# Moving the early weight loads behind ScalarE gates, the warming products onto a zero block, and one fence copy to ScalarE, in a fused linear-attention and MLP kernel

## The chip, the cores and the metric

The kernel runs on one core of a Trainium2 chip. The metric is the device time of one execution in microseconds (us); a profile's span runs from the first to the last instruction of the profiled execution. TensorE is called PE here, VectorE DVE, ScalarE ACT, GpSimd POOL and SyncE SP, as in the profile.

## The reference

Two blocks, one behind the other, all in float32. The first is a recurrence over 768 tokens for 4 batches and 8 heads of 48 channels; the second is an MLP on the 3072 resulting rows of 384 values, with a gate of erf(softplus).

```python
for t in range(S):
    cur = einsum('bhd,bhe->bhde', u * k[t], v[t])
    y[:, :, t] = einsum('bhd,bhde->bhe', r[t], state + cur)
    state = w[t][..., None] * state + einsum('bhd,bhe->bhde', k[t], v[t])
x = y.transpose(0, 2, 1, 3).reshape(B * S, H * D)   # 3072 x 384
h = x @ w_in                                        # 384 x 2048
g = h * erf(log(1 + exp(h)))
out = g @ w_out                                     # 2048 x 384
```

## The kernel before, in words

The work is cut into 12 steps. A step is 128 tokens of two batches: 16 (batch, head) units, kept as 8 pairs on 128 partitions. The order of the instructions on all five engines is written out by hand (`tc.manual_schedule`); each engine runs its own list strictly in that order, and a semaphore is waited for where data or a buffer comes from another engine.

Within a step the token-by-token recurrence is done by halving: for each of six levels PE makes 64 small products (L718, `level_products`) of scaled r and k, DVE scales the halves of r and k in place by the running products of w (L358 and L365, `scale`; step 0 has its own last form, L377), and the masked result is put into `own` (L728 and L735 `take_level`; in step 0 L983, L749 and L1022). The running products of w are made by POOL (L403). Then `own` times v is added into the PSUM tile `y` (L762, `from_own`, once per `swap`), with a small copy of `y` between the two calls as a fence (`fence`, L771, into `seen`). k is transposed by PE, copied to `kT` (L1047 in step 0, L1172 later) and multiplied by v for the state; `middle` is the state after half a step (L1056, L1192, L1196). `through_state` adds r times state (L788), and brings `y` to the MLP's input `xT`: in step 0 by way of `y3` (L797), three products with a placement matrix (L804, the function `hop`) and three ACT copies (L810); in step 1 by copies (L816) and small DMAs (L822).

The MLP of step s-1 runs on PE between the levels of step s. `hidden` makes two blocks of the hidden layer per piece, 12 records of x times w_in (L1268), and ACT copies them out of PSUM (L1277); there are two PSUM buffers for that. Piece n needs the n-th pair of blocks of w_in.

The weights are float32 numbers that come as 64-bit words and are converted on the way: 8 pairs of blocks for w_in, then 8 for w_out, numbered 0 to 15. `convert` gives each pair five stages:

- `l`, `load`: two DMAs of 384 KB by SP (L181) into one of three `words` buffers. With an argument `behind`, one element is first written into the buffer from that tile, by ACT (L273) or POOL (L275), and the DMA waits for it: this is the gate.
- `b`, `scale_high` on ACT (L290, for w_out L292), which for pairs from 2 on uses the PSUM tile `y` as scratch; `r`, `scale_low` on ACT (L298) into `rest`.
- `h`, `shift` on DVE (L307, for w_out also L312), and `o`, `add` on POOL (L320). `j` is `h` and `o` together.

`send(what)` runs the next pair through the named stages, with a counter for each stage. In step 1 it is called behind the first level's products and then at `place(n)`, which stands behind each level, by the row of `CONVERT` for the step.

Before the change the loads stand so: pair 0 at the start, pair 1 in step 0 at level 4 behind a POOL gate, pairs 2 and 3 and v of step 1 at the end of step 0 behind `seen` and `middle` on ACT, pair 4 in `hop`, pair 5 and the w of step 2 in `pending` (step 1, level 2), the others at places 2, 3, 4 and 5 of step 1 without a gate; the r and k of step 2 behind levels 3 and 4 (L1165). The r, k, v and w of step 1 are loaded by `load_second` and L988, L1008 in step 0.

Some products on PE are never read: `stay_warm` (L1085, six times at the start on the identity matrix, twice in step 0) and `keep_busy` (L1094, in each level of step 0). They fill PE where it would wait.

Of the kernel before, what the change touches and what calls it, by code (L numbers as in the profile page):

```python
# [22 lines left out]
NC = 2  # L23
# [68 lines left out]
def kernel(  # L92
# [161 lines left out]
    def convert(weights):  # L254

        held = {}
        plain = weights[0][1].dtype == FP32
        signed = len(weights) // 2  # L260

        def load(i, behind=None, by_scalar=False):
            if i >= len(weights):
                return
            dst, src = weights[i]
            if plain:
                nc.sync.dma_start(out=dst, in_=src)
                return
            words = wide.tile([P, 2, DM, 2], I32, name="words", bufs=3)
            if behind is not None:  # L270
                to = words[:, 0, 0, 0:1].bitcast(FP32)
                if by_scalar:
                    nc.scalar.copy(to, behind)  # L273
                else:
                    nc.gpsimd.tensor_copy(out=to, in_=behind)  # L275
            load_halves(words[:].rearrange("p i n two -> p i (n two)"), src.bitcast(I32))
            held[i] = {"words": words}

        def scale_high(i, part=slice(0, 2)):


            if i not in held:
                return
            if i < 2:
                base = weights[i][0][:, part]
            else:
                base = y[:].rearrange("p e q j t -> p e (q j t)")[:, :, :DM]
            high = held[i]["words"][:, part, :, 1].bitcast(FP32)
            if i < signed:
                nc.scalar.activation(base, high, AF.Prelu, scale=2.0**-112, alpha=-(2.0**32))  # L290
            else:
                nc.scalar.mul(out=base, in_=high, mul=2.0**-112)  # L292
            held[i].setdefault("bases", []).append((base.bitcast(I32), part))

        def scale_low(i):
            if i in held:
                rest = wide.tile([P, 2, DM], I32, name="rest", bufs=2)
                nc.scalar.mul(  # L298
                    out=rest[:], in_=held[i]["words"][:, :, :, 0].bitcast(U32), mul=2.0**-29
                )  # L300
                held[i]["rest"] = rest

        def shift(i):
            if i in held:
                base, part = held[i]["bases"].pop(0)
                into = weights[i][0].bitcast(I32)[:, part]
                nc.vector.tensor_scalar(  # L307
                    out=into if i < signed else base, in0=base, scalar1=3, scalar2=None,
                    op0=ALU.logical_shift_left,
                )  # L310
                if i >= signed:
                    nc.vector.scalar_tensor_tensor(  # L312
                        out=into, in0=held[i]["words"][:, part, :, 1], scalar=-(1 << 31),
                        in1=base, op0=ALU.bitwise_and, op1=ALU.bitwise_or,
                    )

        def add(i):
            if i in held:
                into = weights[i][0].bitcast(I32)
                nc.gpsimd.tensor_tensor(  # L320
                    out=into, in0=into, in1=held.pop(i)["rest"][:], op=ALU.add
                )

        def join(i):
            shift(i)
            add(i)

        stages = {"l": load, "b": scale_high, "r": scale_low, "h": shift, "o": add, "j": join}
        done = {"l": 6, "b": 2, "r": 2, "j": NT // 2}

        def send(what):
            for stage in what:
                stages[stage](done[stage])
                done[stage] += 1

        return stages, send
# [429 lines left out]
                            skip_group_check=True,  # L766
                        )

    def fence():

        nc.vector.tensor_copy(  # L771
            out=seen[:].rearrange("p (e g t) -> p e g t", e=NE, g=NP),
            in_=y[:].rearrange("p e q j t -> p e (q j) t")[..., HC - 1 : HC + 1],
        )

    def through_state(s, xT):
# [18 lines left out]
        y3 = att.tile([P, UNIT], FP32, name="y3", bufs=1)  # L795
        copy = nc.vector.tensor_copy if s == 1 else nc.scalar.copy
        copy(y3[:].rearrange("p (j t) -> p j t", j=NJ), y[:, 1, 1])  # L797
        parts = y[:, 0, 0], y[:, 0, 1], y[:, 1, 0]
        by_kk = [xT[:, kk, :].rearrange("p (j t) -> p j t", j=NJ) for kk in range(KT)]
        if not s:  # L800

            def hop():
                for kk in range(KT):
                    nc.tensor.matmul(  # L804
                        parts[kk], lhsT=apart[:, kk],
                        rhs=y3[:].rearrange("p (j t) -> p j t", j=NJ),
                        start=False, stop=True, skip_group_check=True,
                    )
                for kk in range(KT):
                    nc.scalar.copy(by_kk[kk], parts[kk])  # L810
                stages["l"](4, xT[:, KT - 1, 0:1], True)

            turns["hop"] = hop
            return
# [142 lines left out]
    def attend_first(xT):  # L957


        for _ in prepare(0):  # L960
            pass
        totals = plan_totals(0)
        c, _, vt, made, S, S_next, ends = parts_of(0)
        t5 = turns["first"]
# [25 lines left out]
        for level in range(2, LOG):  # L990
            pp = turns.pop("pp", None) or products([P, NE, JP, HC])
            for j, half in enumerate(halves):
                level_products(pp, first_pair, level, half)
                scale(0, level, batch=j)
            turns["pp"] = products([P, NE, JP, HC])
            keep_busy(turns["pp"], (DM,))
            (take_blocks if level == MASKED else take_level)(own, pp, level)
            wait_for(1 << level - 1)
            if level == 2:
                totals(2)  # L1000
            else:
                totals(*behind[level])
            if level == 2:
                stages["b"](0)
                stages["r"](0)
            if level == 3:
                nc.scalar.copy(ws[1][:, 0, 0:1], t5[:, 1, 0, NP - 1, 4:5])
                nc.sync.dma_start(out=ws[1][:], in_=rkw[1][:, 2])  # L1008
                second = prepare(1)
                next(second)  # L1010
            if level == LOG - 2:
                stages["l"](1, ready[0][1][LOG - 1][:, 0:1])
        totals = plan_totals(1)
        pp = turns.pop("pp")
        for j, half in enumerate(halves):
# [4 lines left out]
        half = HC // 2  # L1020
        for s0, copy in ((0, nc.scalar.copy), (HC, nc.vector.tensor_copy)):
            copy(own[s0 : s0 + half, :, half:], got[s0 : s0 + half, :, :half])  # L1022
        wait_for(0, 1)
        next(second)

# [22 lines left out]
        stages["h"](0)  # L1048
        state_of(0, halves[0], sums[0])
        from_own(0, own, 1)  # L1050
        fence()
        state_of(0, halves[1], sums[1])
        from_own(0, own, 0)
        for j, copy in enumerate((nc.scalar.copy, nc.vector.tensor_copy)):
            n = slice(j * NP, (j + 1) * NP)
            copy(middle[both, n], sums[j][both, n, :D])  # L1056
        stages["l"](2, seen[:, 0:1], True)
        stages["l"](3, middle[:, JP - 1, 0:1], True)
        load_v(1)
        stages["o"](0)  # L1060
        nc.gpsimd.tensor_mul(faded[1][:], middle[:], ends[:, :, 1:2].to_broadcast([P, JP, D]))
        through_state(0, xT)
# [8 lines left out]
        def pending():  # L1071
# [1 line left out]
            state_of(1, range(JP), part)  # L1073
            nc.vector.tensor_add(S_next[both], faded[1][both], part[both, :, :D])
            load_third()
            stages["l"](5)
            load_w(2)

        turns["pending"] = pending

    def stay_warm(times):

        for _ in range(times):
# [2 lines left out]
                ps[:], lhsT=ident[:], rhs=ident[:, None, :].to_broadcast([P, NC, P]),  # L1086
                start=True, stop=True,
            )

    def keep_busy(pp, columns=(DM, DM // 2)):  # L1090

# [7 lines left out]
    def attend(s, xT, early, place, behind):  # L1099
# [11 lines left out]
        for level in range(near_log(s) + 1 if s == DIRECT else 1, LOG + 1):  # L1111
            rk = by_pair(made) if level == 1 else RK
            pp = turns.pop("pp", None) or products([P, NE, JP, HC])
            if s == level == 1:
                level_products(pp, rk, level, range(NP))
                turns.pop("hop")()
                level_products(pp, rk, level, range(NP, JP))
                send("br")
            elif s != 2 or level != 2:
                level_products(pp, rk, level)  # L1120
            if level == LOG and s == DIRECT:
# [39 lines left out]
            if (s, level) == (DIRECT - 1, LOG - 1):  # L1161
                nc.gpsimd.tensor_copy(out=first[:, 0:1], in_=own[:, 0, HC // 4 : HC // 4 + 1])
                mixing.send(nc.gpsimd)
            if s == 1 and level in (3, 4):
                nc.sync.dma_start(out=loaded[2][0][:, level - 3], in_=rkw[2][:, level - 3])  # L1165

        from_own(s, own, 1)
        ps = products([P, JP, P])
# [7 lines left out]
        if c:  # L1176
            nc.gpsimd.tensor_mul(
                faded[0][:], S[:], ends[:, :, 0:1].to_broadcast([P, JP, D])
            )
        next(following, None)  # L1180
        place(LOG)
        if s == 2:
# [408 lines left out]
    def run_late(s, tokens, following=None):  # L1591
# [36 lines left out]

    CONVERT = (
        (),  # L1630
        (("", "br"),) * 2 + (("", "brl"),) * 3 + (("", "l"), ("", ""), ("", ""), ("", "brl")),
        (("", "jbrl"),) * 4 + (("", "jl"), ("", ""), ("", ""), ("", ""), ("", "br")),
        (("", "jbr"), ("j", "br"), ("j", "")),
    )
# [6 lines left out]
    joining, mixing_tokens = shared_weights(), shared_tokens()  # L1641
    mixing = mix_weights()
    next(mixing)
    make_identity(nc, ident[:])
    nc.vector.memset(y[:], 0.0)
    nc.vector.memset(sums[:], 0.0)
# [10 lines left out]
    with tc.manual_schedule(  # L1657
        engines={getattr(mybir.EngineType, x) for x in ("PE", "DVE", "Activation", "Pool", "SP")}
    ):
        stay_warm(6)  # L1660
        for t in (*states[0], *states[1], middle):
            nc.gpsimd.memset(t[:], 0.0)
        nc.gpsimd.memset(over_blocks[:], 1.0)
        nc.scalar.copy(u_row[:, :1], ident[:, :1])
        stages, send = convert(
# [7 lines left out]
        for s in range(n_steps):  # L1673
# [7 lines left out]
            def place(n):  # L1681
# [7 lines left out]
                if s in ALONE:  # L1689
                    if s == 2 and not n:  # L1690

                        next(hids[0])
                        turns.pop("ahead")()
                    convert_at(n)
                    if (s, n) == (1, LOG - 1):
                        load_w(3)
                        load_v(2)
# [146 lines left out]
```

## Time and profile before

| | |
|---|---|
| time, median of 3 runs | 568.98 us (568.19 to 570.46) |
| the profiled execution: time | 569.04 us |
| the profiled execution: span | 567.3 us |
| PE busy | 560.0 us, 99% of the span |
| DVE, ACT, POOL busy | 453.7, 357.5, 245.1 us |
| moved by DMA | 63.24 MB, mean 111 GB/s |
| step 0, step 1 | to about 24 us, about 24 to 55 us |

A line of a timeline or of the groups reads: start, duration, engine, source line, operation, tile written and tile read, shapes, count, and in brackets the engine's idle time ahead of it with what ended it. In the chain of waits each line is a start, a duration and the work that the end depended on; "issue" is time in which the engine waited for nothing that the profile shows. Ends of products are modelled.

### The profile page before, as it was taken

How to read it: one execution, taken by the hardware profiler on the slowest of the kernel's cores; microseconds unless marked ns; L12 is line 12 of the kernel's file. 1: busy time of each engine (PE TensorE's matmuls, PEld its weight loads, DVE VectorE, ACT ScalarE, POOL GpSimd, SP SyncE). 2: the span in 40 equal slices, each digit the busy share in tenths (PEclk: the TensorE clock that was granted, in tenths of full speed). 3: DMA queues.
4: the chain of work that ended last, by engine and by line, in shares of the span. 5: the costliest groups of instructions: out<-in, count | busy, mean ns of one | idle time of the engine just before them, and what ended most of it. 6: DMA issues, size and time to landing. Idle time of an engine off the chain costs nothing.

```text
span 567.3 us, 16701 instructions
## 1 busy us (share of the span) xinstructions
PE 560.0 (99%) x7314; PEld 500.0 (88%) x7314; DVE 453.7 (80%) x513; ACT 357.5 (63%) x491; POOL 245.1 (43%) x261
## 2 busy tenths in 40 slices
PE   8999999999999999999999999999999999999997
PEld 6778886688998998998998998898899899989997
DVE  8885986999899998799889789689688587477910
ACT  4667787655458858747756765766676771489500
POOL 3875381733885883393484185176073000000000
PEclk9999999999999999999999999999999999999999
DMA  7793662350435325245145235235332301000000
GB/s 272 241 383 136 250 201 84 157 159 4 148 86 169 110 66 166 37 166 164 29 137 187 38 130 194 39 113 168 49 112 84 47 9 35 3 2 0 29 29 28
DMA packets 54081, 63.24 MB, mean 111 GB/s; under 512 B 35160, under 2 KB 40568, under 8 KB 52984
## 3 DMA queue, kind: packets, MB, share of 16 engines
q1 hardware_dynamic: 53480, 61.98, 34.8%
q8 instruction: 57, 0.93, 0.7%
q10 hardware_dynamic: 528, 0.20, 0.2%
q14 instruction: 16, 0.13, 0.1%
HBM read 52.39 MB, written 8.69 MB: 108 GB/s over the span
## 4 chain that ended last, share of the span: by engine, by line
PE 97%; DVE 1%; DMA 1%; issue 0%; ACT 0%; DVEq 0%; ACTq 0%
PE m L1268 37%; PE m L1390 36%; PE c L1493 6%; PE pp L718 6%; PE m L1300 4%; PE y L762 2%; PE y L788 2%; PE pp L836 2%; DMA in<-in_rkw 1%; PE pp L1170 1%; PE pp L1094 1%; PE c L1390 0%; PE pp L849 0%; PE y L804 0%; DVE own L728 0%
## 5 line engine op out<-in xcount | busy, mean ns | idle before, releaser
L1268 PE MATMUL m<-xT,w_in_sb 128*128 128x256 f32 x960 | 214.0, 381 | 0.0
L1268 PEld LDWEIGHTS m<-xT,w_in_sb 128*128 128x128 f32 x960 | 180.3, 190 | 24.4
L365 DVE TENSOR_TENSOR in<-in,tot_sb 128x1024 f32<-128x1024 f32 (+1 forms) x55 | 76.2, 1385 | 9.1 <-PE pp L718 8.0
L1277 ACT COPY h<-m 128x512 f32<-128x512 f32 x80 | 46.3, 581 | 54.0 <-PE m L1268 53.9
L1390 PE MATMUL m<-mixed,h 128*128 128x192 f32 x320 | 56.7, 331 | 0.0
L1390 PE MATMUL m<-w_out_sb,h 128*128 128x192 f32 x320 | 56.1, 329 | 0.0
L1390 PEld LDWEIGHTS m<-mixed,h 128*128 128x128 f32 x320 | 51.8, 190 | 0.8
L1390 PEld LDWEIGHTS m<-w_out_sb,h 128*128 128x128 f32 x320 | 52.0, 190 | 0.5
L1390 PE MATMUL m<-w_out_sb,room 128*128 128x192 f32 x288 | 49.7, 326 | 0.0
L1390 PEld LDWEIGHTS m<-w_out_sb,room 128*128 128x128 f32 x288 | 47.3, 190 | 0.1
L520 POOL TENSOR_TENSOR words<-words,own 128x384 f32<-128x384 f32 x21 | 30.4, 1445 | 26.5 <-DVE words L551 13.0
L718 PEld LDWEIGHTS pp<-in 48*48 48x48 f32 (+4 forms) x2368 | 30.4, 120 | 11.6 <-issue 6.1
L1228 ACT ACT_TABLE_LOAD x28 | 35.9, 1283 | 7.2 <-DVE h L1233 6.8
L561 POOL TENSOR_TENSOR words<-words 128x384 f32<-128x384 f32 x28 | 38.7, 1411 | 0.0
L513 POOL TENSOR_TENSOR own<-rest 128x384 f32<-128x384 f32 x7 | 8.1, 1151 | 68.4 <-ACT o L1396 68.4
L1224 ACT ACT_TABLE_LOAD x28 | 35.9, 1283 | 1.8 <-issue 1.3
L718 PE MATMUL pp<-in 48*48 48x32 f32 (+4 forms) x2368 | 34.3, 206 | 1.0 <-issue 1.0
L465 POOL TENSOR_TENSOR tot_sb<-tot_sb 128x256 f32<-128x256 f32 (+4 forms) x50 | 31.6, 631 | 3.8
L586 DVE TENSOR_REDUCE sums<-rk 128x16 f32<-128x768 f32 (+2 forms) x31 | 31.3, 1022 | 0.0
L561 POOL TENSOR_TENSOR rk<-words 128x384 f32<-128x384 f32 x28 | 30.6, 1122 | 0.0
L1224 ACT ACTIVATE room<-h 128x1024 f32<-128x1024 f32 x28 | 29.6, 1057 | 0.3
L320 POOL TENSOR_TENSOR w_out_sb<-w_out_sb,rest 128x768 int32<-128x768 int32 x8 | 17.5, 2181 | 22.5 <-DVE w_out_sb L312 22.5
(226 smaller groups left out, 1008.6 us busy)
## 6 DMA issues: line engine op xcount, KB each, us to landing
in<-in_rkw SPq DMA_DIRECT2D x8, 1024.0 KB, 5.4
words<-in_moe_w_in SPq DMA_DIRECT2D x16, 384.0 KB, 5.8
words<-in_moe_w_out SPq DMA_DIRECT2D x16, 384.0 KB, 6.7
words<-in_rk_rows SPq DMA_DIRECT2D x8, 768.0 KB, 7.4
w<-in_rkw SPq DMA_DIRECT2D x11, 512.0 KB, 7.0
v<-in_v SPq DMA_DIRECT2D x12, 384.0 KB, 5.4
out<-o SPq DMA_DIRECT2D x23, 192.0 KB, 2.9
in<-in_rkw SPq DMA_DIRECT2D x7, 512.0 KB, 4.7
```

The source lines that it names most:

```text
L365: nc.vector.tensor_mul(halves, halves, view(tots[level - 1], 0, [[1, n], [2, nb], [0, half]]))
L465: nc.gpsimd.tensor_mul(new, pair[:, :, 0], pair[:, :, 1])
L520: engine.tensor_mul(to, to, of[:, :, None, :].to_broadcast([P, NEAR // 2 // half, half, D]))
L561: engine.tensor_mul(to[:, i], r[:, half:], k[:, part * rows + i, None].to_broadcast([P, half, D]),)
L586: nc.vector.tensor_reduce(out=to, in_=of, axis=mybir.AxisListType.X, op=ALU.add)
L718: nc.tensor.matmul(to, lhsT=rk(1, n)[rows(e), s0 : s0 + m], rhs=right, start=True, stop=True,)
L1224: nc.scalar.activation(sp_room, chunks[0], AF.Softplus)
L1228: nc.scalar.activation(at, sp_room, AF.Erf)
L1268: nc.tensor.matmul(ps[:, ff, :], lhsT=w_in_sb[:, g * FG + f + ff, kk * P : (kk + 1) * P], rhs=xT[:, kk, :], start=kk == 0, stop=kk == KT - 1,)
L1277: nc.scalar.copy(h[:, f : f + FT, :], ps[:])
L1390: nc.tensor.matmul(to, lhsT=a[:, f], rhs=b[:, f], start=start and f == 0, stop=f == FG - 1, skip_group_check=True,)
L1493: nc.tensor.matmul(to[:, f], lhsT=turns["weights"][b][:, i * FT + f], rhs=turns["tokens"][a], start=a + b in STARTS and not f, stop=True, ...
```

## The change

- The six unread products at the start run on a block of zeros, which POOL clears ahead of the identity matrix, with 116 columns instead of 128. A seventh product, zeros times the first scaled r, is put behind the preparation of step 0. The block is the first 128 columns of a state tile, whose other columns are cleared later.
- `fence` takes the copying engine as an argument; the first step's fence is copied by ACT.
- Pair 1 is loaded behind the last column of `own` by an ACT gate, ahead of the `kT` copies of step 0; pair 2 behind `y3`, pair 3 behind `xT` in `hop`. Pairs 4 to 8 are loaded by a new stage `g`: the same load, with an ACT gate behind the newest `rest`; pair 9 behind `kT` of step 1.
- The w of step 2 is loaded at place 0 of step 1, its r at place 1, its k and the v of step 1 at place 3, k behind an ACT gate.

```diff
             if behind is not None:
-                to = words[:, 0, 0, 0:1].bitcast(FP32)
+                to = words[:, 0, 0, 0:1]
+                to = to.bitcast(FP32) if behind.dtype == FP32 else to
                 if by_scalar:
                     nc.scalar.copy(to, behind)
...
-        done = {"l": 6, "b": 2, "r": 2, "j": NT // 2}
+        done = {"l": 4, "b": 2, "r": 2, "j": NT // 2}
 
-        def send(what):
+        def last_rest():
+            return held[done["r"] - 1]["rest"][:, 0, 0:1]
+
+        turns["last_rest"] = last_rest
+
+        def send(what, behind=None):
             for stage in what:
+                if stage == "g":
+                    load(done["l"], last_rest() if behind is None else behind, True)
+                    done["l"] += 1
+                    continue
                 stages[stage](done[stage])
                 done[stage] += 1
...
-    def fence():
+    def fence(copy=nc.vector.tensor_copy):
 
-        nc.vector.tensor_copy(
+        copy(
...
         copy(y3[:].rearrange("p (j t) -> p j t", j=NJ), y[:, 1, 1])
+        if not s:
+            stages["l"](2, y3[:, 0:1], True)
...
                 for kk in range(KT):
                     nc.scalar.copy(by_kk[kk], parts[kk])
-                stages["l"](4, xT[:, KT - 1, 0:1], True)
+                stages["l"](3, xT[:, KT - 1, 0:1], True)
...
         for _ in prepare(0):
             pass
+        warm_up(1)
...
-            if level == LOG - 2:
-                stages["l"](1, ready[0][1][LOG - 1][:, 0:1])
...
             copy(own[s0 : s0 + half, :, half:], got[s0 : s0 + half, :, :half])
+        stages["l"](1, own[:, NH - 1, HC - 1 : HC], True)
         wait_for(0, 1)
...
         from_own(0, own, 1)
-        fence()
+        fence(nc.scalar.copy)
         state_of(0, halves[1], sums[1])
...
-        stages["l"](2, seen[:, 0:1], True)
-        stages["l"](3, middle[:, JP - 1, 0:1], True)
-        load_v(1)
...
             load_third()
-            stages["l"](5)
-            load_w(2)
...
+    WARM = 116
+
+    def warm_up(times):
+
+        for _ in range(times):
+            ps = ps_m.tile([P, NC, WARM], FP32, name="m")
+            rhs = zeros[:, None, :WARM].to_broadcast([P, NC, WARM])
+            if not times - 1:
+                rhs = ready[0][0][:, 0, :NC, :WARM]
+            nc.tensor.matmul(ps[:], lhsT=zeros, rhs=rhs, start=True, stop=True)
...
-                send("br")
+                send("brg")
...
-            if s == 1 and level in (3, 4):
-                nc.sync.dma_start(out=loaded[2][0][:, level - 3], in_=rkw[2][:, level - 3])
...
+        if s == 1:
+            send("g", kT[:, 0, 0:1])
         next(following, None)
         place(LOG)
...
-        (("", "br"),) * 2 + (("", "brl"),) * 3 + (("", "l"), ("", ""), ("", ""), ("", "brl")),
+        (("", "brg"),) * 3 + (("", "br"), ("", "brg")) + (("", ""),) * 3 + (("", "brl"),),
...
+    zeros = states[1][1][:].rearrange("p n d -> p (n d)")[:, :P]
+    nc.gpsimd.memset(zeros, 0.0)
     make_identity(nc, ident[:])
...
-        stay_warm(6)
-        for t in (*states[0], *states[1], middle):
+        warm_up(6)
+        for t in (*states[0], states[1][0], middle):
             nc.gpsimd.memset(t[:], 0.0)
+        nc.gpsimd.memset(states[1][1][:].rearrange("p n d -> p (n d)")[:, P:], 0.0)
...
                     convert_at(n)
+                    if (s, n) == (1, 0):
+                        load_w(2)
+                    if (s, n) == (1, 1):
+                        nc.sync.dma_start(out=loaded[2][0][:, 0], in_=rkw[2][:, 0])
+                    if (s, n) == (1, 3):
+                        nc.scalar.copy(loaded[2][0][:, 1, 0, 0:1], turns["last_rest"]())
+                        nc.sync.dma_start(out=loaded[2][0][:, 1], in_=rkw[2][:, 1])
+                        load_v(1)
```

## The prediction

> **What bounds the kernel now.** I read the page's engine totals, then the idle time of PE by stage, then the chain of waits where PE was idle, then the engine timelines of that stretch.
>
> ```profile
> PE 560.0 (99%) x7314; PEld 500.0 (88%) x7314; DVE 453.7 (80%) x513; ACT 357.5 (63%) x491; POOL 245.1 (43%) x261
> 0.00:17.00 17.00, 14.60 (x348) 10.40 (x348) 15.11 (x28) 8.02 (x21) 6.47 (x23) 1.00 0.79 265
> 17.00:24.00 7.00, 6.29 (x239) 5.33 (x238) 4.59 (x10) 4.11 (x10) 5.95 (x10) 1.00 0.64 178
> 24.00:48.00 24.00, 23.03 (x458) 18.94 (x456) 20.23 (x19) 16.95 (x29) 20.32 (x21) 1.00 0.98 367
> 48.00:62.00 14.00, 13.90 (x333) 11.69 (x333) 8.08 (x13) 10.41 (x15) 4.33 (x6) 1.00 0.22 69
> ```
>
> The columns of the last four lines are the stage, its length, busy time of PE, PEld, DVE, ACT, POOL, then granted clock, DMA share, GB/s. PE is idle 7.3 us in all (567.3 less 560.0) and 4.2 us of it falls before 62 us: 2.4 to 17, 0.7 to 24, 1.0 to 48, 0.1 to 62. From 62 to 560 us PE is busy 498.0 of 498.0 us, and the other 3.1 us of idle time is the tail behind the last products. So every edit of this change, all of them before 62 us, can move the end only by moving the time at which PE gets through step 1; whatever is lost there is lost for good, and the most that could be won is these 4.2 us, of which the first 1.7 (no product before the identity is made) and most of the step-0 waits are not touched.
>
> ```profile
> 20.05 0.91 DVE w_in_sb L307
> 20.96 0.09 DVE seen L771
> 21.10 0.66 PE y L762 x32
> 36.82 0.97 issue
> 48.11 0.59 PE y L762 x32
> ```
>
> Two removable places: PE waits at 21.10 for the fence, which DVE runs only after a 0.99 us shift, and at 36.82 PE stands 0.97 us for nothing that the profile shows, in a stage whose DMA share is 0.98. Now ScalarE, which the change loads with new gates:
>
> ```profile
> 17.98 0.57 ACT L1022 COPY own<-pp 32x512 f32<-32x512 f32 x1 [0.33 <-PE pp L718]
> 18.74 0.48 ACT L1047 COPY kT<-m 128x384 f32<-128x384 f32 x1 [0.18 <-PE m L1033]
> 22.28 0.37 ACT L797 COPY y<-y 128x256 f32<-128x256 f32 x1 [0.69 <-PE y L788]
> 22.55 0.91 ACT L290 ACTIVATE w_in_sb<-words 128x768 f32<-128x768 f32 x1
> 24.30 0.92 ACT L810 COPY xT<-y 128x256 f32<-128x256 f32 x3
> 29.13 0.88 ACT L290 ACTIVATE y<-words 128x768 f32<-128x768 f32 x1 [1.47 <-DMA words<-in_moe_w_in]
> 45.37 1.18 ACT L735 COPY own<-pp 32x512 f32<-32x512 f32 x2
> 18.77 0.69 DVE L1022 COPY own<-pp 32x512 f32<-32x512 f32 x1
> ```
>
> Conversion 1 starts at 22.55 right behind the arrival of its load (issued 17.46 and 17.84, landed 20.97 and 22.44 by the landing events), and the level-6 copies end at 46.55, 1.5 us ahead of the products at 48.04 that need them. Those two margins, 0.1 and 1.5 us, decide.
>
> **The change, part by part.** Write l, b, r for load, high and low conversion of weight pair n.
>
> *First products on zeros.* The 128-column zero block is one 0.2 us memset ahead of the identity, so PE can start near 1.0 instead of 1.68. Six products are 12 records at 427 ns apart before; 116 columns instead of 128 make them 387, so they end near 5.7. The added single product waits for the first scaled r (DVE, 5.80) and ends by 6.6, where the first useful products start because ScalarE ends the last rk copy at 6.55 after the landing at 5.1. Cost and gain nothing in this profile: the record spacing falls from 427 to 217 ns near 5.8, ahead of 6.6 (the clock column shows 1.00 from the start and has no entry for this). If the full rate came later in some executions, the first 64 products (1.19 us) would run up to twice as long, so the earlier start is worth 0 to 0.6 us there; I take 0. "TensorE: Matmul & The Clock Gate" in the Trainium skill (Part 1) says the full clock comes after a busy window of some 3.4 us that runs freely and is not reset by the first product; the trace agrees as far as one run can (4.1 us after the first product). By that rule the change would fall anywhere between 3.4 and 6.8 us after the new start, which alters no term here.
>
> *Load 1 behind own.* It leaves POOL (0.53 us, which nobody waited for) and goes to ScalarE between its L1022 copy (end 18.55) and its kT copy. The gate reads the last column on all partitions, so it waits for DVE's half too (end 19.46). Queued behind it on ScalarE: the kT copy, fence, middle, everything. Gate 0.19 (as L273), kT copy from 19.7 to 20.2 instead of 19.22: the state products start 0.9 later. From there PE has 1.4 us of work (state 0.45, own 0.57, state 0.45) and the ScalarE fence (0.17) runs inside the last piece, so the second L762 batch starts at 21.6 instead of 21.10: +0.5. The fence's own gain, had the kT copy stayed, is 21.10 less 20.7, 0.4; it is spent here. Hop 23.2 to 24.75 instead of 22.70 to 24.26.
>
> *Load 1's landing.* Issued at 19.7 instead of 17.46. A pair of halves issued to an idle queue took 4.27 and 4.34 us from first issue to second landing (issued 70.35 and 74.37), and 4.98 where the second issue itself took 1.52 instead of 0.43 (17.84). With 4.3 it lands at 24.0; b1 and r1 (1.8) end at 25.8, and the xT copies, in order behind them, start at 25.8 instead of 24.30. PE's first hidden products start at 26.15 instead of 24.85: **+1.3** on PE (0.5 from the gate, 0.8 from the load).
>
> *Loads 2 to 7 behind ScalarE.* Each pair's gate is two conversions ahead, so ScalarE and the loads become one loop. xT copies end 26.7; gate, l3 issued 26.95, landed 31.25; b3, r3 to 33.05; gate, l5 issued 33.25, landed 37.55; behind it on the queue w of step 2 (512 KB, 1.3 us at the 406 GB/s of 38 to 42 us) and l6 (two halves at 0.97), landed 40.8 instead of 38.39. From there ScalarE is never idle: b6 r6 1.8, gate 0.2, hidden copy 0.55, the scaled r of step 2 2.0, b7 r7 1.8, gate 0.2, copy 0.55, level-6 copies 1.2, sum 8.2, end 49.0. The products at 48.04 start at 49.05: **+1.0**. PE's own chain comes to the same place: +1.3, less 0.15 that it waited for DVE at 35.97, is 49.15 if the 0.97 stall returns and 48.2 if it goes. The later of the two chains sets the end, so the stall's removal, bounded by 0 and 0.97, is worth nothing here.
>
> *SP's late issues.* Of the 32 issues before 62 us that move 384 KB or more, four took over 1 us (17.84, 22.19, 35.48, 57.27). Six issues stand on the loop, so 0.75 of them should be late, at 0.7 each: +0.5. From none to three late: 0 to +2.1.
>
> *Moved, no cost.* v of step 1 is issued near 43.7 behind the half of step 2's input, lands by 47.4 and is needed at 49.0: 1.6 of cover; if SP is held, PE waits what is beyond it. Step 2's r lands 42.1, needed by ScalarE at 43.3. l8, w of step 3, v of step 2 and l9 go to the stretch from 48, where the DMA share was 0.22; l9 must be out of the way of the xT transfers at 56, which it is by calculation (55.9), and 1.9 us late at most if not. The gate on kT is 0.19 on an engine that then has 0.5 us before it is needed.
>
> Sum: +1.0 +0.5 = **+1.5** on the profiled execution's 569.04 (span 567.3 and 1.8 around it); that stands 0.06 over the median of the runs, 568.98. Forecast **570.5**.
>
> **Rivals.**
> *The loads bind harder (slower over the bound).* Same loop, but with two or three late issues, or with landings of the loaded kind (7.1 us median from 24 to 48). At 5.3 us a pair instead of 4.3, the three links l1, l3, l5 give +3.0 over the +1.0, 573.0. For it: the loop has no cover. Against: the queue is emptier by construction, and the 7.1 is backlog. It decides from 4.9 us a pair on, where the sum passes +2.85. "DMA: Bandwidth & Descriptors" in the Trainium skill (Rules for kernel authors) advises to issue a transfer early and wait late, which is against gating; the waits of 1.3 to 1.5 us for loads in this trace already show arrival as the limit of ScalarE.
> *The gates cost nothing and the reliefs count.* If the own gate let the kT copy pass (a wait for ScalarE's half only), and landings took 3.9 a pair, the fence's 0.4 and the stall's 0.97 remain: -1.4, 567.7. For it: DMA share 0.98 around the stall. Against: the gate's column lies in both halves, and the instruction order is strict.
> *The zeros do not bring the full clock.* Then the first 64 products and the two after cost up to twice their 1.19 and 1.13, +1.5 on the forecast, 572.0. Against: the present warming operand is zero off the diagonal.
>
> **How the numbers follow.** Forecast 0.52, harder loop 0.21, reliefs 0.23, cold start 0.04. Forecast's own range 569.5 to 571.8. A measurement of this kernel tells about 0.5%, 2.85 us, from no change; that is 566.1 and 571.8 around the median. Faster by more needs the reliefs and the 0.6 of an early clock and more: 0.05. Slower: the harder loop and the cold start, less what of both stays under: 0.21. Within: 0.74. The range takes the reliefs with an early clock at the bottom, 567.0, and the harder loop at the top, 573.0; beyond them I leave 2 in 10.
>
> **What would show it.** Right: in the changed profile the kT copy of ScalarE starts near 19.7 behind a gate that waited for DVE's L1022; conversion 1 starts near 24 with a DMA wait; the first hidden products near 26.1; ScalarE without a gap from 41 to 49; the L762 products of step 1 near 49; nothing changed after 62. Wrong: kT copy still at 18.7, or hidden products before 25, or L762 before 48 (the reliefs), or a PE wait for v or for own over 2 us (the harder loop), or record spacing of 400 ns after 6.6 us (the clock).

## The result and the profile after

The changed kernel took 572.95 us (median; 572.15 to 573.92) against 569.26 us (568.19 to 570.46) for the kernel before on the same chip: a ratio of 1.0065 [1.0049, 1.0082], 3.7 us slower, at the edge of the 0.5% that a measurement of this kernel can tell. Forecast 570.5, range 567.0 to 573.0. The time is inside the range, but it is the harder loop's (573.0) and not the forecast's. All ratios below compare undisturbed executions with those of the kernel before that ran in the same series; they are not quotients of the medians given beside them.

The profiled execution took 573.03 us with a span of 571.2, 3.9 more than before. Engine totals of the page, and then the stages to 62 us (the same stretches, the same columns):

```profile
PE 560.9 (98%) x7316; PEld 500.6 (88%) x7316; DVE 451.6 (79%) x512; ACT 359.1 (63%) x499; POOL 242.7 (42%) x261
```

```profile
0.00:17.00 17.00, 14.53 (x346) 10.62 (x346) 14.87 (x28) 7.85 (x20) 6.36 (x23) 1.00 0.80 264
17.00:24.00 7.00, 5.08 (x233) 4.29 (x232) 4.18 (x8) 2.70 (x9) 4.26 (x9) 1.00 0.34 98
24.00:48.00 24.00, 21.78 (x456) 17.83 (x450) 17.99 (x17) 16.36 (x33) 17.49 (x19) 1.00 0.81 258
48.00:62.00 14.00, 13.37 (x281) 10.95 (x269) 6.88 (x11) 11.39 (x19) 6.21 (x8) 1.00 0.72 243
```

PE is idle 2.5, 1.9, 2.2 and 0.6 us in the four stages, 7.2 in all against 4.2 before. The moved loads are visible in the DMA share: 0.34 instead of 0.64 in the second stage, 0.72 instead of 0.22 in the fourth. The first hidden products start at 27.38 instead of 24.82 (+2.56), the first of step 1's own products at 50.84 instead of 48.04 (+2.8), and the hidden products before 62 us at 63.43 instead of 59.49 (+3.94). The three places in PE's timeline before, and the two of them after that do not stand further down:

```profile
24.82 2.86 PE L1268 MATMUL m<-xT,w_in_sb 128*128 128x256 f32 x12
48.04 0.67 PE L762 MATMUL y<-own,v 64*48 64x64 f32 x32
59.49 5.45 PE L1268 MATMUL m<-xT,w_in_sb 128*128 128x256 f32 x24
50.84 0.32 PE L772 MATMUL y<-own,v 64*48 64x64 f32 x4
63.43 2.86 PE L1286 MATMUL m<-xT,w_in_sb 128*128 128x256 f32 x12
```

From there nothing more is lost: the span is 3.9 longer. 3.0 us of it are idle time, 0.9 busy time.

What PE waited for before 64 us, where it differs most from before (line; what ended the wait; us in all, times, longest):

```profile
PE pp L728 <- issue: 1.7, 3, 0.7
PE pp L728 <- DVE in L375: 1.4, 1, 1.4
PE pp L1053 <- ACT kT L1059: 0.9, 1, 0.9
PE y L772 <- ACT own L745: 0.2, 1, 0.2
```

PE's own timeline has these waits in their places:

```profile
18.14 0.73 PE L728 MATMUL pp<-in 48*32 48x32 f32 x61 [0.71 <-issue]
22.49 0.67 PE L772 MATMUL y<-own,v 64*48 64x64 f32 x32
26.81 0.45 PE L728 MATMUL pp<-rk 48*64 48x64 f32 x12 [0.66 <-issue]
27.38 2.83 PE L1286 MATMUL m<-xT,w_in_sb 128*128 128x256 f32 x12
39.98 1.03 PE L728 MATMUL pp<-in 48*56 48x32 f32 x64 [1.42 <-DVE in L375]
51.35 0.65 PE L772 MATMUL y<-own,v 64*48 64x64 f32 x28 [0.20 <-ACT own L745]
```

The stall of 0.97 us that stood at 36.82 is gone. In its stead are three shorter ones of the same kind (0.71, 0.66, and 0.33 at 59.62), and a wait of 1.42 us for DVE's level-4 input. ScalarE:

```profile
20.55 0.19 ACT L274 COPY words<-own 128x1 f32<-128x1 f32 x1 [1.04 <-DVE own L1033]
20.64 0.47 ACT L1059 COPY kT<-m 128x384 f32<-128x384 f32 x1
25.24 0.95 ACT L291 ACTIVATE w_in_sb<-words 128x768 f32<-128x768 f32 x1 [0.97 <-DMA words<-in_moe_w_in]
33.05 0.90 ACT L291 ACTIVATE y<-words 128x768 f32<-128x768 f32 x1 [2.07 <-DMA words<-in_moe_w_in]
36.94 0.86 ACT L291 ACTIVATE y<-words 128x768 f32<-128x768 f32 x1 [1.42 <-DMA words<-in_moe_w_in]
50.13 1.17 ACT L745 COPY own<-pp 32x512 f32<-32x512 f32 x2
```

The gate waits for DVE's half of `own` as the prediction had it, conversion 1 waits for its load, and two later conversions wait 2.07 and 1.42 us for theirs (before, none waited longer than 1.54 for its load). The level-6 copies end at 51.30, 4.75 us later than before. The chain of waits of the same stretch shows why (start, duration, what; parts left out):

```profile
24.67 4.36 DMA words<-in_moe_w_in
29.06 0.87 ACT y L291
29.93 0.84 ACT rest L299
30.79 0.20 ACT words L274
31.01 0.33 SPq L181
31.39 5.44 DMA words<-in_moe_w_in
36.94 0.87 ACT y L291
...
38.71 1.22 DVE in L375
...
41.32 1.71 DVE in L375
43.03 0.63 DVE own L738
...
43.68 0.90 ACT y L291
...
51.35 0.65 PE y L772 x28
```

This is the loop in one reading: pair 2 lands, ScalarE makes its two conversions, only then the gate releases the load of pair 4, which takes 5.8 us from first issue to second landing; DVE's part of level 4 is in order behind that pair, and PE behind DVE. From there the chain goes on over DVE's levels 4 and 5 to conversion 6, which starts at 43.68, just behind DVE's `own` (43.66); pair 6 landed at 43.57, so the two paths meet there within 0.1 us. Before, the chain's step at 36.82 was PE's own stall, with no load in it.

### The profile page after: what moved, and what is told of

The parts are those of the page before. It is cut to its first block, busy times and chain, and to the rows that moved or that the text cites. A ratio compares the mean times of both kernels' runs of the same rounds, so it can differ in the third digit from the quotient of the medians.

```text
span 571.2 us, 16711 instructions
## 1 busy us (share of the span) xinstructions
PE 560.9 (98%) x7316; PEld 500.6 (88%) x7316; DVE 451.6 (79%) x512; ACT 359.1 (63%) x499; POOL 242.7 (42%) x261
## 4 chain that ended last, share of the span: by engine, by line
PE 93%; DMA 3%; DVE 2%; ACT 1%; issue 1%; SPq 0%; DVEq 0%; ACTq 0%
PE m L1408 35%; PE m L1286 34%; PE c L1511 6%; PE pp L728 5%; PE m L1318 4%; PE y L772 2%; PE y L798 2%; DMA words<-in_moe_w_in 2%; PE pp L848 2%; DVE in L375 1%; DMA in<-in_rkw 1%; PE pp L1186 1%; PE pp L1112 1%; ACT y L291 1%; DVE own L738 1%
```

## The experiments

**Which part makes the loss?** The gates of the stage `g` alone, in the kernel before:

```diff
-        done = {"l": 6, "b": 2, "r": 2, "j": NT // 2}
+        done = {"l": 4, "b": 2, "r": 2, "j": NT // 2}
...
+                if stage == "g":
+                    load(done["l"], last_rest() if behind is None else behind, True)
...
-                stages["l"](4, xT[:, KT - 1, 0:1], True)
...
-            stages["l"](5)
...
-        (("", "br"),) * 2 + (("", "brl"),) * 3 + (("", "l"), ("", ""), ("", ""), ("", "brl")),
+        (("", "brg"),) * 3 + (("", "br"), ("", "brg")) + (("", ""),) * 3 + (("", "brl"),),
```

> The kernel before with the gates alone: pairs 4 to 9 loaded behind rest and kT at the places of the changed kernel, all other loads, the warming products and the fence as before. If the gates behind rest cost by themselves: 571 to 571.8 us, with a wait of PE for DVE ahead of a level. If they cost only because pairs 1 to 3 are late already: under 569.7 us.

574.21 us, ratio 1.0074 [1.0049, 1.0099]: this one edit, in the kernel before, costs as much as the whole change, and more than was expected. From PE's waits between 16 and 56 us:

```profile
PE y L772 <- ACT own L745: 2.7, 2, 2.5
PE pp L728 <- DVE in L375: 0.5, 1, 0.5
```

and from ScalarE's timeline:

```profile
41.24 0.95 ACT L291 ACTIVATE y<-words 128x768 f32<-128x768 f32 x1 [2.53 <-DMA words<-in_moe_w_in]
45.80 1.32 ACT L452 ACTIVATE rk<-in,u_sb 128x128 f32<-128x128 f32 x4 [2.31 <-DMA in<-in_rkw]
49.82 1.17 ACT L745 COPY own<-pp 32x512 f32<-32x512 f32 x2
```

Nothing is left of PE stalls without a cause here, and there is a loss all the same. ScalarE waits 2.53 and 2.31 us for transfers (the second is the r of step 2, queued behind a late pair), its level-6 copies end at 50.99, and PE stands 2.5 us before step 1's products. The granted clock of the stage that follows, 48 to 62 us, is 0.88 instead of 1.00, and that is a part of this run's loss: the products behind step 1's own ones (line 1178) start 3.0 us later than before (51.63 against 48.64), and what follows the twelve hidden products is 4.7 us late (56.92 against 52.25). Nine of its ten executions have a mean clock of 0.997 or less, as two of six of the changed kernel have; more on that below.

The other way round, the changed kernel with the same loads at the same places, but without the gates of the stage `g`:

```diff
-                    load(done["l"], last_rest() if behind is None else behind, True)
+                    load(done["l"])
```

> The changed kernel, with pairs 4 to 9 loaded at the same places in SP's list but without the ScalarE gates, as soon as their buffer is free. Theory B (the gates behind rest delay loads 4 and 6, and PE's wait of 1.4 us for DVE before level 4 is theirs): the loads of pairs 4 and 5 are issued 2 us earlier, that wait is gone, 571.3 to 571.7 us. Theory A: what is lost before 28 us stays, loads 2 and 3 are late anyway, and the gates cost under 0.5 us: 572.5 to 573 us.

570.44 us, 1.0019 [1.0004, 1.0034]: 2.5 us come back, more than was expected. Pair 4 is issued at 27.17 instead of 31.01, PE waits for no DVE input before level 4, and step 1's own products start at 49.05 instead of 50.84.

Pair 1 alone behind `own`, in the kernel before:

```diff
-            if level == LOG - 2:
-                stages["l"](1, ready[0][1][LOG - 1][:, 0:1])
...
+        stages["l"](1, own[:, NH - 1, HC - 1 : HC], True)
```

> The kernel before with pair 1 loaded behind own by ScalarE, ahead of the kT copy, and nothing else. The prediction's two terms: kT copy 0.9 us later, second batch of own times v 0.5 us later, first hidden products 1.3 us later: 570.3 us. If the gates behind rest are needed to make it count: 569.3 us.

569.67 us, 1.0007 [0.9984, 1.0029]: this run alone cannot tell the predicted 1.3 us (a ratio of 1.0023) from nothing. The pair is issued at 19.92 and lands at 24.16. From PE's timeline:

```profile
26.39 2.83 PE L1267 MATMUL m<-xT,w_in_sb 128*128 128x256 f32 x12 [0.22 <-ACT xT L810]
37.50 1.03 PE L718 MATMUL pp<-in 48*56 48x32 f32 x64
38.46 2.86 PE L1267 MATMUL m<-xT,w_in_sb 128*128 128x256 f32 x12
48.36 0.67 PE L762 MATMUL y<-own,v 64*48 64x64 f32 x32
```

The first hidden products are 1.6 us late (predicted 1.3) and level 4 is still 1.5 late at 37.50. But in this execution the 0.97 stall is not there, and the next hidden products start only 0.3 late (38.46 against 38.13). One profile cannot say that the one took the place of the other.

Two variants of the changed kernel with pair 1 elsewhere. First, back at its old place (POOL's gate at level 4):

```diff
+            if level == LOG - 2:
+                stages["l"](1, ready[0][1][LOG - 1][:, 0:1])
...
-        stages["l"](1, own[:, NH - 1, HC - 1 : HC], True)
```

> The changed kernel, with pair 1 alone loaded as before (POOL gate at level 4 of step 0, no gate on own). Theory A (the chain that starts with the gate on own: ScalarE waits for DVE's half of own, and pair 1 lands some 2.7 us later) expects the kT copy of ScalarE right behind its own copy, conversion 1 without a DMA wait, the first hidden products 1.3 to 2 us earlier than in the changed kernel (27.4), and 571.0 to 571.7 us. Theory B (the loss is made by the later loads behind rest) expects the first hidden products earlier as well, but PE waiting longer for DVE before level 4, and 572.5 to 573 us. Theory C (PE's stalls without a shown cause, 1.7 us in the changed kernel up to 60 us) expects no order in it: whatever stalls remain, 572 to 573 us.

571.5 us, 1.0040 [1.0021, 1.0058]. The difference to the full change (1.0065) is 1.4 us, and the intervals overlap. Its profiled execution was the slowest of its twelve (575.38). Its first hidden products are at 28.07, later than in the changed kernel and not earlier as expected, because PE stood 0.80 and 1.68 us without a shown cause ahead of them. Behind that, PE's timeline shows the loop:

```profile
36.43 2.86 PE L1287 MATMUL m<-xT,w_in_sb 128*128 128x256 f32 x12
41.17 1.03 PE L728 MATMUL pp<-in 48*56 48x32 f32 x64 [1.88 <-DVE in L375]
42.13 4.54 PE L1287 MATMUL m<-xT,w_in_sb 128*128 128x256 f32 x12
```

With pair 1 early, pair 4 still took 5.96 us (32.06 to 38.02), PE waited 1.88 us, and the twelve products after it took 4.54 us instead of 2.86, because the granted clock stood at half from 43.06 to 46.47. Here pair 6 had landed at 44.47, and conversion 6 waited on for DVE's `own`, to 44.92.

Second, the own gate behind ScalarE's `kT` copy instead of ahead of it, so that step 0 does not wait for the gate:

```diff
-        stages["l"](1, own[:, NH - 1, HC - 1 : HC], True)
...
+        stages["l"](1, own[:, NH - 1, HC - 1 : HC], True)
```

> The changed kernel, with the gate on own put behind ScalarE's kT copy instead of ahead of it. The gate still waits for DVE's half of own, so the load is issued at nearly the same time, but the kT copy does not wait. Theory A, if the blocked ScalarE is what costs: 0.5 us less, 572.4 us. If the late landing of pair 1 is what costs: the state products 0.9 us earlier, the first hidden products where they were (27.4), and 572.9 us.

572.91 us, 1.0064 [1.0040, 1.0087]: nothing gained. The products that read `kT` came at 19.55 in this run, against 20.35 in the run without the gates of `g`, where the own gate still stood ahead of the copy; the first hidden products came at 26.39 against 26.53, each 0.51 us after the `xT` copies began, which stand behind conversion 1. So the block on ScalarE was lifted, and it hardly mattered: the start of step 1 is set by the load and not by the `kT` copy.

Both undone in the changed kernel: pair 1 at its old place, and the loads of the stage `g` without their gates. The zeros, the seventh product, the fence, the new places of the other loads, the gates of pairs 2 and 3 (behind `y3` and `xT`) and the one on step 2's k stay.

```diff
-                    load(done["l"], last_rest() if behind is None else behind, True)
+                    load(done["l"])
...
+            if level == LOG - 2:
+                stages["l"](1, ready[0][1][LOG - 1][:, 0:1])
...
-        stages["l"](1, own[:, NH - 1, HC - 1 : HC], True)
```

> The changed kernel with both undone: pair 1 loaded as before, and pairs 4 to 9 without the gates behind rest. The warming products, the ScalarE fence and the new places of the other loads stay. If the late loads are the whole loss (1.4 us for pair 1, 2.5 us for the gates by the runs so far): 569.0 to 569.5 us, the time of before. If the fence or the warming products cost something by themselves, as the fence alone at 570.7 us hints: 570.3 us or more.

568.97 us, 0.9988 [0.9964, 1.0012]: the whole loss is gone, and the rest of the change is worth nothing measurable. The later places of pairs 2 to 9, of w, r, k and v by themselves cost nothing that shows. Four runs, all with the rest of the change in place and each compared with its own series, make a table with two sides:

| | pair 1 at its old place | pair 1 behind `own` |
|---|---|---|
| pairs 4 to 9 without gates | 568.97 us (0.9988) | 570.44 us (1.0019) |
| pairs 4 to 9 with gates | 571.5 us (1.0040) | 572.95 us (1.0065) |

Read down, the gates cost 2.5 us in both columns, and the intervals do not overlap. Read across, pair 1 costs 1.4 to 1.5 us in both rows; there the intervals overlap a little, so this is an estimate. It is the size that the prediction gave pair 1 (+1.3).

**Is it the loop?** If the delay is that a load is released only after two conversions, then a gate put ahead of the two conversions must give most of it back while everything else stays. It copies from a constant tile (`first`) that was written long before, so only its place in ScalarE's order holds the load:

```diff
-                    load(done["l"], last_rest() if behind is None else behind, True)
+                    load(done["l"], first[:, 0:1] if behind is None else behind, True)
...
-                send("brg")
+                send("gbr")
...
-        (("", "brg"),) * 3 + (("", "br"), ("", "brg")) + (("", ""),) * 3 + (("", "brl"),),
+        (("", "gbr"),) * 3 + (("", "br"), ("", "gbr")) + (("", ""),) * 3 + (("", "brl"),),
```

> The changed kernel with each gate of pairs 4 to 8 ahead of the two conversions at its place instead of behind them (a gate on a tile that is long written; only ScalarE's order holds it). If ScalarE and the loads form a loop (gate, landing, conversion, next gate), taking the 1.8 us of two conversions and their wait for the landing out of it frees it: pair 4 issued near 28 us instead of 31.0, the level-6 copies end by 49.5 instead of 51.3, 570.3 to 571 us. If the places of the loads in SP's list cost, and not the loop: 572.5 us or more.

570.97 us, 1.0019 [1.0002, 1.0037], as without these gates. The copies that make the gates, some 0.2 us of ScalarE each, are all still there, so it is not they that cost. Pair 4 is issued at 27.37 (31.01 in the changed kernel), PE does not wait for DVE before level 4, and ScalarE's level-6 copies end at 49.77 instead of 51.30:

```profile
48.60 1.17 ACT L745 COPY own<-pp 32x512 f32<-32x512 f32 x2
```

**The parts that were put at nothing.** The zeros and the seventh product alone, then the fence alone, then both, in the kernel before:

```diff
+        warm_up(1)
...
-        stay_warm(6)
+        warm_up(6)
```

> The kernel before with the warming products on zeros alone (six with 116 columns, started behind the zero block, and the seventh behind the scaled r). The prediction's term is 0: 569.0 us, with the first useful products at the same time. The rival on zeros (products that do not bring the full clock): the spacing of PE's records stays near 400 ns beyond 7 us, 570.5 us or more. An earlier full clock in the executions where it comes late: 568.5 us, and fewer times above 570.5 us.

568.88 us, 0.9989 [0.9966, 1.0012].

```diff
-        fence()
+        fence(nc.scalar.copy)
```

> The kernel before, with the first step's fence copied by ScalarE and nothing else. The prediction's term: PE's second batch of own times v starts at 20.7 instead of 21.10, 0.4 us gained, 568.9 us. The rival: the middle copies and hop follow at their old times, 569.3 us; below 568.6 us the fence would free more than its wait.

570.72 us, 1.0022 [0.9999, 1.0045]: inconclusive, with a spread of 568.55 to 574.04. The profiled execution had three stalls without a cause (1.12, 1.67 and 0.53 us) in its first 29 us, so the 0.4 that the prediction gave the fence cannot be read from it.

> The kernel before with the two parts of the change that gate no load: the warming products on zeros (two-column products left out again) and the ScalarE fence. If the fence's 0.4 us and an earlier full clock are both real: 568.2 us, 0.15% under the kernel before, which these rounds can hardly tell from none. If the fence alone was slower (570.7 us) because of itself and not because of PE's stalls and the late clock of those executions: 570 us or more.

568.6 us, 0.9999 [0.9977, 1.0020]. Together they are worth nothing that can be measured; that the fence alone looked slower was not repeated beside the zeros.

**What are the stalls without a cause?** In the profiles that have them they stand at the same places in PE's order of records: 705, 961, 1217, 1473, 1729, 2497, which is 256 k + 193. The page's queue list has the code: 57 packets, 0.93 MB, 16 KB each. PE has 14,715 records in the changed kernel, 258 to a packet, so a packet seems to be 256 records of 64 bytes (an estimate). In the changed kernel the last such packets ahead of the stalls start at 15.96, 24.34 and 57.53, and the stalls end at 18.14, 26.81 and 59.95, 2.2 to 2.5 us later; in the kernel before one starts at 35.22, and the stall ends at 37.79. To test it, 48 records were put ahead of all useful work in the kernel before (twelve unread products of two columns, behind the changed kernel's products on zeros): if the stalls belong to the code, they stay at their counts and the work under them moves.

```diff
+        tiny = ps_m.tile([P, NC, P], FP32, name="m")
+        for _ in range(12):
+            nc.tensor.matmul(tiny[:, 0, :2], lhsT=zeros, rhs=zeros[:, :2], start=True, stop=True)
```

> The kernel before with the warming products on zeros, and 12 more products of 2 columns behind the six (48 more records of PE), which nobody waits for. PE's stalls without a shown cause stood 193 records past a multiple of 256 in every profile so far (705, 961, 1217, 1729, 2497). If the place is one in PE's code, and not in the work, stalls stand at the same counts, hence 24 products earlier in the work: the one at 961 in the products ahead, the one at 1217 in hop, where they cost less; 568.3 us. If it is in the work, they stay in the half-state and level-1 products, at counts 48 higher.

> The same with the first step's fence on ScalarE too: the version that takes of the change what does not gate a load. If the fence's 0.4 us shows once the stalls are moved: 567.9 us, 1.1 us under the kernel before. If not: as the one without the fence, 568.3 to 568.9 us.

The second of them has ScalarE's fence as well. Its stalls, in PE's timeline:

```profile
27.08 1.02 PE L804 MATMUL y<-y,mixed 128*128 128x256 f32 x4 [0.54 <-issue]
33.30 0.56 PE L1042 MATMUL pp<-v,kT 64*48 64x48 f32 x17 [0.38 <-issue]
```

They are at counts 1217 and 1473. In seven of the other profiles, the changed kernel's among them, the stall at 1217 is in the level products behind the hop (26.81 above, the last 12 of 32); here, at the same count, it is in the hop itself (line 804), 48 records earlier in the work. So the stalls go with the count and not with the work, which is what the loading of PE's code would do; that it is this loading is inferred from the counts and the packets, and no run takes the loading away. The times were a surprise: 578.08 us (1.0154 [1.0125, 1.0184]) and 577.0 us (1.0108 [1.0071, 1.0145]). From the first one's stages:

```profile
6.00:10.00 4.00, 4.00 (x66) 3.43 (x69) 2.62 (x9) 1.10 (x5) 1.27 (x3) 0.70 0.91 339
10.00:28.00 18.00, 17.82 (x365) 12.17 (x359) 10.73 (x16) 5.75 (x14) 3.26 (x13) 0.50 0.49 155
```

The clock column is 0.50 from 10 to 28 us, with PE 99% busy: after the small products the full clock was withdrawn at 7.64 for 20.48 us. In the profile of the second, its fastest execution (572.23), it was withdrawn at 9.15 for 3.41 us. So these two runs say nothing about the cost of a stall, only about its place.

## Why the prediction was right and wrong

**First products on zeros: 0.** Right: 0.9989 alone. The full clock was there at 4.60, 3.6 us after the first product, on an operand of nothing but zeros; so the rival on zeros is out.

**The own gate: +0.5 on the second batch.** Right in mechanism. The batch is at 22.49, 1.39 late; of that 1.05 is DVE's half of `own` starting later already (19.82 against 18.77: the first products started 0.22 later with the first landing, and the 0.71 stall came in level 6), so 0.34 is the gate, less the 0.40 wait for the fence that is gone. The prediction had the `kT` copy near 19.7 from an undisturbed start; it is at 20.64.

**Load 1's landing, 4.3 a pair, +1.3 on the first hidden products.** Right: the landing took 4.40 here, 4.24 in the run with pair 1 alone, which gave +1.6, and 1.4 to 1.5 us of time by the table. In the changed kernel the products start at 27.38 and not at the forecast 26.15, because the load was issued at 20.76 and not at 19.7, with the late `own`. The stall of 0.66 ended at 26.81, ahead of the `xT` copies (26.89), and cost nothing there.

**The loop, +1.0: the step that failed.** The mechanism was right, and the runs show it (gates taken out, or put ahead of the conversions: 2.0 to 2.5 us back). Its size was off by 2.3 us: level-6 copies to 51.30 instead of 49.0. The failing term is the 4.3 us a pair. Those rows were read from an empty queue far from step 1. In the profile of the changed kernel the pairs took (first issue to second landing):

| pair | issued | landed | us |
|---|---|---|---|
| 1 | 20.76 | 25.16 | 4.40 |
| 2 | 24.29 | 29.04 | 4.75 |
| 3 | 28.01 | 32.95 | 4.94 |
| 4 | 31.01 | 36.83 | 5.82 |
| 5 | 35.05 | 39.39 | 4.34 |
| 6 | 38.88 | 43.57 | 4.69 |

Also, the prediction walked the odd pairs (1, 3, 5) and took pair 6 from the queue behind pair 5; the chain that ended last goes over pairs 2 and 4. At 4.3 a pair both walks give nearly the same: 24.29 + 4.3, 1.97 from landing to the next first issue, 4.3, 2.05, 4.3 is 41.2, against 40.8 in the prediction. The three measured pairs are 2.36 longer than 3 x 4.3 (0.45, 1.52, 0.39), which is 43.57. From there to the end of the level-6 copies are 7.73 us (8.2 predicted; its terms add up to 8.3), so 0.4 of start, 2.36 of landings and -0.47 of ScalarE's work make the 2.3. Pair 6's 0.39 is not decisive, though. The prediction walked ScalarE alone, and DVE stands in the loop too: held by pair 4, its levels 4 and 5 end at 43.66, so conversion 6 would have started no earlier with a shorter landing. ScalarE was to be without a gap from 41 to 49 and waited 1.72 us there, up to 43.68.

The mean of the even pairs is 5.1, beyond the 4.9 from which the harder loop was to decide. By that rival's own sum 5.1 gives 572.4; that the time is so close to its 573.0 is in part luck, for 0.6 of the 3.9 us came in behind the loop, with the stall at 59.62. Its sign, a PE wait of over 2 us for v or `own`, came only in the run with the gates alone (2.45); here that wait is 0.20. Its chance of 0.21 was too low for a loop whose landings were all taken at the price of an empty queue. PE's own chain, the other of the two in the prediction, holds a misreading: the 0.15 us that PE is said to have waited for DVE at 35.97 is no wait in the profile, since these products follow the group ahead of them at the usual 2.79 us.

**The 0.97 stall, worth 0.** The number held, for a reason that was not seen. The stall is not there in the changed kernel's profile, but such stalls stand at counts of PE's records, and three others came, 1.7 us in all. Which of them appear differs from profile to profile, at fixed counts: they are not something that a moved load removes.

**SP's late issues, +0.5.** The size is fair: one issue took over a microsecond (28.39, 1.53, the second half of pair 3), but on the chain that ended last it was pair 2's second half that was late, 0.95 instead of 0.43. That half microsecond is in pair 2's 4.75 already. The prediction counted it beside the pairs, and left the 4.98 that it had read for a pair with a late issue out of a pair's price.

**Moved, no cost.** The v of step 1 was issued at 46.04 instead of the forecast 43.7, landed at 50.66 and was needed at 50.84: 0.2 of cover and not 1.6. In the run with the gate behind the `kT` copy PE waited 0.5 for it. After 64 us nothing more was lost, as predicted.

**Open.** Why pair 4 took 5.8 (5.96 with pair 1 early): a code packet of 1.12 us starts at 33.00, within its flight, and one of 1.88 at 33.34 in the run with pair 1 early, but no run takes it away. Neither does any run say why the stall comes at one count in one execution and at another in the next. What the gates do in the kernel before, where they cost more (3.0 us by PE's timeline, besides the clock) than the 2.5 us in the changed kernel, was not taken apart either.

## What to carry to other kernels

A load that is released by an engine which must first consume the loads before it is no longer a transfer in the background: latency, conversions and issue add up in a loop, and in a kernel that its TensorE bounds, as here, a late landing beyond the loop's cover is not won back. Price such a loop with the longest landings of its own stage, and follow every one of its interleaved chains and every engine that stands in it; if a gate is wanted, put it ahead of the consumer's work (here that took the ratio from 1.0065 to 1.0019) or leave the loads in a queue that nothing blocks. Before giving a stall without a cause a price, see whether it stands at the same instruction count in other runs.

## What the runs showed of the hardware

- **A short wait can cost twice.** Three times PE stood still for 1.88, 1.43 and 2.5 us (pair 1 early; gate behind `kT`; gates alone), and each was followed by 3.41 us at half the granted clock, in which a group of twelve hidden products took 1.0 to 1.7 us longer. Others were not (1.67 with the fence alone, 1.42 after, and a second 1.43 in the very run with the gate behind `kT`), so the length alone does not decide. "TensorE: Matmul & The Clock Gate" in the Trainium skill (Why this matters for your kernels) warns of idle gaps of more than about 3 us; here it followed gaps of 1.43 to 2.5 us, and the measurement decides.
- **The clock can be lost after very small products.** With twelve products of two columns put in behind the zeros, the grant was withdrawn at 7.64 for 20.48 us, six times 3.41, with PE busy 99% of the time by the profile from 10 to 28 us.
- **What seems to be code loading shows as "issue".** 16 KB for some 256 records, stalls of 0.3 to 1.7 us at counts 256 k + 193, in some profiles none and in others three. SP's issues of over 1 us start within 0.3 us of such packets, all seven of them before 62 us in the two kernels: 28.39 beside 28.35 and 50.15 beside 50.15 after, 17.84 beside 17.87 and 57.27 beside 57.18 before.
